# A new hand order for the first 36 positions of a fused attention and two-stage feed-forward kernel, on one core

## Chip, cores and metric

The kernel runs on one core of a Trainium2 chip. The metric is the device time of one execution in microseconds (us), as the median of several executions. The kernel before takes 648.68 us, the median of three runs (647.57 to 649.09).

## What is computed

The reference, cut to its three stages:

```python
# attention: 2 batches, 8 heads, 768 positions, head size 64
scores_l = scale * q @ k.T                    # kept where |i - j| < 16
scores_s = scale * q @ k_sum.T + log(32)      # k_sum: maximum of k over blocks of 32
a = softmax(concat(scores_l, scores_s))
attn = a @ concat(v, v_sum)                   # v_sum: mean of v over blocks of 32
x = attn, heads side by side                  # 1536 x 512
# first feed-forward, d_ff 1536
x = ((x @ w_a) * (x @ w_b)) @ w_out
# second feed-forward, d_ff 2048
h = x @ w_in
out = (h - tanh(h)) @ w_out2
```

The weights arrive as 64-bit floats. The chip's engines turn each tile of them into a 32-bit float by integer work, and each matrix product of the feed-forwards runs as three products of a high and a low part.

## The kernel before

The 1536 rows are taken in three blocks of 512. The first feed-forward walks through each block in "positions": one position is a product with one 128-wide slice of w_a (`pos_a`), w_b (`pos_b`) or w_out (`pos_o`), each of 12 matmuls of 512 columns. Attention is made in 24 units of 64 query positions. Block 0 needs units 0 to 7, block 1 units 8 to 15, block 2 units 16 to 23.

The first 36 positions (`HEAD_P = 36`, line 457), the attention of units 0 to 15 and the decoding of the first 36 weight tiles follow an order written out by hand: the string `SEQ` (line 828). Each name is one step, issued by `op` (line 590 on) in that order. Every engine takes its own steps from the string strictly in their order; steps of different engines only wait for the data and the buffers that they share. After the 36th position the rest comes from a planner's due times and a list scheduler.

Steps on TensorE (PE): `Kt` and `KP` transpose k, `T1t` q, `T2m` makes scores (8 matmuls), `vm` the block means of v, `T3t` transposes the weights of a unit, `T4m` multiplies them with v (16 small matmuls), `Mp0_0` to `Mp35_3` are the quarters of the 36 positions (3 matmuls each).
Steps on ScalarE (ACT): `Ke` evacuates k, `ex` the exponentials, `T4h` the high part of the attention output, `da`/`db` the first two of the decoding steps of a weight tile, `sh` its high part, `Ma`/`Mh` evacuations of positions.
Steps on VectorE (DVE): `Kr` the block maxima of k, `tt` mask and maximum, `rb` the reciprocal of a unit's sum, `T4l` the low part of the attention output, `dd`/`de` (and mostly `df`) the further decoding steps, `Mt`/`Ml`.
For the steps in the table `EC` (line 567) the engine is chosen by a letter (A, D or P for ACT, DVE and GpSimd, which the profile calls POOL): copies of q (`T1ea`, `T1eb`), of k windows (`W`), of transposed weights (`T3e`), the scaling `nm`, copies of the v means `vc`, the decoding step `dc`, the low part `sl` of a weight.
Loads: `LK`, `Lq`, `Lv`, `LV`, `Lk` on the queue of SyncE (SP) for k, q and v; `Lw` for the next weight tile, into one of five staging buffers, when step `df` of an earlier tile has freed it.

A weight's chain is thus `Lw`, `da`, `db`, `dc`, `dd`, `de`, `df`, `sh`, `sl`, and then its position. The first position needs all of `T4h0..7` and `T4l0..7` too, since each product runs over all 512 rows of the block.

PSUM tiles are taken in rotation: eight tags until the eighth unit (`tg`), after that two (`tg2`), so `KP0` takes the place of an earlier `T4m` and waits for its `T4h` and `T4l`.

Dummies: `warm(n, d)` (line 582) puts matmuls that nobody reads ahead of a step. For each unit in `PACED[n]` it issues a small product that reads that unit's sums (so it waits for `rb`) and six transposes of the identity; `FILL[n]` adds single transposes. The steps `T1t`, `T2m`, `T3t` and `T4m` call it; `KP` doesn't:

```python
        elif k == "KP":
            t = knat.pop((1, i))
            pp = pt(tg2(), (128, NP, 128))
            for p in range(NP):
                nc.tensor.transpose(pp[:, p, :], t[:, 2 * p : 2 * p + 2, :], ident)
            P_["KP", i] = pp
```

Of the kernel before, what the change touches and what calls it, by code (L numbers as in the profile page):

```python
# [39 lines left out]
def band_attention_moe_kernel(ctx: ExitStack, tc: tile.TileContext, q, k, v, w_a, w_b, w_out, w_in, w_out2, out):  # L40
# [3 lines left out]
    B, H, S, D = q.shape  # L44
# [530 lines left out]

    qbs = [qbd, qbd2, qbd3, qbd4]
    P_A, P_B = ([j for j in range(HEAD_P) if pos[j][0] is fn] for fn in (pos_a, pos_b))
    FILL = {'KP0': 3}

    SM, PACED = {}, {'T3t0': [5, 3, 0, 1], 'T3t2': [2], 'T3t6': [4], 'T3t7': [6], 'T3t1': [7]}  # L580

    def warm(n, d):
        for u in PACED.get(n, ()):
            mm(d[0:NP, :], SM[u], ident, start=True, stop=True)
            for _ in range(6):
                nc.tensor.transpose(d, ident, ident)  # L586
        for _ in range(FILL.get(n, 0)):
            nc.tensor.transpose(d, ident, ident)

    def op(n):  # L590
# [3 lines left out]
        i, c = int(i or 0), int(c or 0)  # L594
        e = EC.get(n, "A")
        if k == "LK":
# [170 lines left out]
        elif k in ("dc", "dd", "de", "df"):  # L767
# [117 lines left out]
```

## Time and profile before

| | us |
|---|---|
| median of three runs | 648.68 |
| the profiled execution itself | 649.94 |
| its span, first to last instruction | 648.2 |
| TensorE busy in the span | 638.0 (98%) |
| VectorE busy | 499.6 (77%) |
| ScalarE busy | 474.3 (73%) |
| GpSimd busy | 193.4 (30%) |

The span is what the trace covers. Of the profiled execution 1.7 us lie around it. The ends of matmuls in the trace are modelled, so a row of TensorE that overlaps the next is read by its start: the distance from one start to the next is what a step took. The row of a step with three starts or more gives the first start and the end of the last.

### The profile page before, as it was taken

Reading aid. Unit: us, or ns where it says so; the run is one execution under the profiler, and the core shown is the slowest. Engines: PE = TensorE matmul, PEld = TensorE weight load, DVE = VectorE, ACT = ScalarE, POOL = GpSimd, SP = SyncE. Lnnn points to the kernel's source line nnn. Section 1 sums busy time; section 2 is a strip of 40 time slices with the busy share of each in tenths; the row PEclk is TensorE's granted clock in tenths of the full one; section 3 lists DMA queues with packets and bytes.
Section 4 is the critical chain, followed back from the end, with each engine's and each line's share of the span. In section 5 each row is a group of like instructions: output and inputs, shape, how many; then the busy total and the mean of one; then the engine's idle time right before and its main releaser. Section 6 shows DMA issues by size and latency. Waiting matters only on the chain.

```text
span 648.2 us, 9696 instructions
## 1 busy us (share of the span) xinstructions
PE 638.0 (98%) x3296; PEld 521.4 (80%) x3296; DVE 499.6 (77%) x1019; ACT 474.3 (73%) x998; POOL 193.4 (30%) x206
## 2 busy tenths in 40 slices
PE   6999999999999999999999999999999999999997
PEld 5787888778888888888888888888888888888885
DVE  4989999989764777657877748877777877777775
ACT  4889999897676887546555558777777777777774
POOL 5632221110000111001111143544444544444441
PEclk9999999999999999999999999999999999999999
DMA  9979996554514345423444100000010000100001
GB/s 203 252 199 262 252 253 200 173 166 121 148 41 134 123 127 145 143 92 120 147 147 146 34 1 1 0 1 1 2 66 0 1 1 1 50 16 1 1 1 65
DMA packets 81678, 62.12 MB, mean 96 GB/s; under 512 B 45716, under 2 KB 72340, under 8 KB 81628
## 3 DMA queue, kind: packets, MB, share of 16 engines
q1 hardware_dynamic: 79276, 60.32, 33.4%
q0 software_dynamic: 2352, 1.18, 1.5%
q8 instruction: 26, 0.43, 0.3%
q14 instruction: 24, 0.20, 0.1%
HBM read 54.00 MB, written 7.34 MB: 95 GB/s over the span
## 4 chain that ended last, share of the span: by engine, by line
PE 94%; DVE 2%; DMA 2%; SPq 1%; issue 0%; DVEq 0%
PE acc L439 20%; PE pb L350 15%; PE pa L350 15%; PE acc L378 10%; PE acc L802 5%; PE pt L350 5%; PE ps L350 5%; PE pb L808 5%; PE pa L808 4%; PE ps L268 2%; DMA w<-in_q_dram 1%; DMA x20a<-in_q_dram 1%; SPq L597 1%; PE ps L320 1%; PE acc L586 1%; PE pt L268 1%
## 5 line engine op out<-in xcount | busy, mean ns | idle before, releaser
L185 POOL TENSOR_TENSOR wsp<-w,wsp 128x512 fp32r<-128x512 f32 x97 | 127.4, 1331 | 140.1 <-ACT wsp L184 137.7
L184 ACT ACTIVATE wsp<-w 128x512 fp32r<-128x512 f32 x165 | 99.1, 621 | 13.6 <-PE acc L378 8.0
L439 PE MATMUL acc<-wsp,gh 128*128 128x512 f32 x256 | 78.8, 389 | 0.0
L179 POOL TENSOR_SCALAR w<-w 128x512 f32<-128x512 f32 x37 | 25.6, 693 | 171.4 <-ACT w L154 81.4
L185 DVE TENSOR_TENSOR wsp<-w,wsp 128x512 fp32r<-128x512 f32 x68 | 48.6, 715 | 35.8 <-ACT wsp L184 35.5
L378 PE MATMUL acc<-gh,wsp 128*128 128x512 f32 x192 | 64.1, 393 | 0.0
L350 PE MATMUL pa<-XB,wsp 128*128 128x512 f32 x240 | 60.6, 396 | 0.0
L350 PE MATMUL pb<-XB,wsp 128*128 128x512 f32 x240 | 60.4, 394 | 0.0
L343 ACT ACTIVATE gh<-tg 128x512 fp32r<-128x512 f32 x56 | 34.9, 623 | 30.6 <-DVE tg L366 30.3
L439 PEld LDWEIGHTS acc<-wsp,gh 128*128 128x128 f32 x256 | 48.1, 188 | 10.0
L350 PEld LDWEIGHTS pb<-XB,wsp 128*128 128x128 f32 x240 | 44.4, 188 | 9.3
L350 PEld LDWEIGHTS pa<-XB,wsp 128*128 128x128 f32 x240 | 44.1, 188 | 9.3
L439 PE MATMUL acc<-wsp,gl 128*128 128x512 f32 x128 | 49.8, 389 | 0.0
L344 DVE TENSOR_TENSOR gl<-tg,gh 128x512 fp32r<-128x512 f32 x56 | 38.5, 687 | 10.5 <-ACT gh L343 10.3
L439 PE MATMUL acc<-wsp,vw 128*128 128x512 f32 x192 | 46.5, 390 | 0.0
L350 PE MATMUL pa<-XA,wsp 128*128 128x512 f32 x192 | 46.1, 389 | 0.0
L350 PE MATMUL pb<-XA,wsp 128*128 128x512 f32 x192 | 46.1, 389 | 0.0
L439 PEld LDWEIGHTS acc<-wsp,vw 128*128 128x128 f32 x192 | 35.9, 188 | 8.2 <-ACT vw L343 0.4
L350 PEld LDWEIGHTS pb<-XA,wsp 128*128 128x128 f32 x192 | 36.0, 188 | 7.5
L350 PEld LDWEIGHTS pa<-XA,wsp 128*128 128x128 f32 x192 | 36.0, 188 | 7.5
L378 PEld LDWEIGHTS acc<-gh,wsp 128*128 128x128 f32 x192 | 35.8, 188 | 7.5
L378 PE MATMUL acc<-gl,wsp 128*128 128x512 f32 x96 | 37.7, 392 | 0.0
(334 smaller groups left out, 1451.2 us busy)
## 6 DMA issues: line engine op xcount, KB each, us to landing
stage<-in_moe_w_out_dram SPq DMA_DIRECT2D x19, 512.0 KB, 3.3
stage<-in_moe_w_in_dram SPq DMA_DIRECT2D x16, 512.0 KB, 4.5
stage<-in_moe_w_a_dram SPq DMA_DIRECT2D x8, 512.0 KB, 5.6
w<-wsc SPq DMA_DIRECT2D x16, 256.0 KB, 3.5
vw<-in_v_dram SPq DMA_DIRECT2D x19, 192.0 KB, 3.0
stage<-in_moe_w_b_dram SPq DMA_DIRECT2D x7, 512.0 KB, 4.8
wsc<-x21a SPq DMA_DIRECT2D x8, 256.0 KB, 4.5
wsc<-x21b SPq DMA_DIRECT2D x8, 256.0 KB, 4.7
```

Of the source, the lines that this page charges most:

```text
L179: eng.tensor_scalar(rf, rf, HI_HI, HI_LO, op0=ALU.min, op1=ALU.max)
L184: nc.scalar.activation(s[:, 0, :], r, AF.Copy)
L185: eng.tensor_tensor(s[:, 1, :], r, s[:, 0, :].bitcast(F32), op=ALU.subtract)
L268: mm(pp[:, p, 0:NK], qt[:, p, :], kw[:, p, :], start=True, stop=True)
L320: mm(pp[h * 64 : (h + 1) * 64, p * 64 : (p + 1) * 64], vt[:, 2 * p + h, :], at[:, p, h * 64 : (h + 1) * 64], start=True, stop=True,)
L343: nc.scalar.activation(dst[0], src, AF.Copy)
L344: eng.tensor_tensor(dst[1], src, dst[0].bitcast(F32), op=ALU.subtract)
L350: mm(dst, w, xx, start=(kk == 0 and n == 0), stop=(kk == KC - 1 and n == 2))
L378: mm(acc[blk][d][:, c0:c1], w, t, start=(f == 0 and c0 == 0 and n == 0), stop=(f == F1 - 1 and n == 2))
L439: mm(a[c], g[:, cs], s[:, i, :], start=(f == 0 and n == 0), stop=(f == F2 - 1 and n == 2))
L802: mm(acc[0][c], w, t, start=(f == 0 and m == 0), stop=(f == F1 - 1 and m == 2))
L808: mm(P_["M", i], w, t, start=(c == 0 and m == 0), stop=(c == KC - 1 and m == 2))
```

## The change

Three things change: the string `SEQ` (the same 838 steps in another order), 28 letters of the table `EC`, and the two tables of dummies. The diff, with the order cut after the first quarters of the sixth position (the first 20 loads, the same in both, are left out):

```diff
-    EC = {
...
-        'T1eb2': 'D', 'W1': 'D', 'W2': 'P', 'nm0': 'D', 'nm2': 'P', 'T3e2': 'A', 'nm3': 'D', 'nm4': 'P', 'T3e4': 'A', 'nm5': 'P', 'T3e6': 'D',
-        'T3e7': 'D', 'vc1': 'D', 'vc2': 'D', 'vc7': 'P', 'dc7': 'D', 'dc12': 'D', 'dc20': 'P', 'dc23': 'D', 'dc25': 'P', 'dc26': 'P', 'dc28': 'D',
-        'dc29': 'P', 'dc33': 'D', 'W9': 'A', 'W11': 'D', 'T1eb4': 'A', 'nm15': 'D',
...
+    EC = {
...
+        'T1eb2': 'A', 'W1': 'P', 'W2': 'D', 'nm0': 'P', 'nm2': 'D', 'T3e2': 'D', 'nm3': 'P', 'nm4': 'D', 'T3e4': 'D', 'nm5': 'D', 'T3e6': 'A',
+        'T3e7': 'A', 'vc1': 'P', 'vc2': 'P', 'vc7': 'D', 'dc7': 'P', 'dc12': 'P', 'dc20': 'D', 'dc23': 'P', 'dc25': 'D', 'dc26': 'D', 'dc28': 'P',
+        'dc29': 'D', 'dc33': 'P', 'W9': 'D', 'W11': 'A', 'T1eb4': 'D', 'nm15': 'A',
...
-    FILL = {'KP0': 3}
-
-    SM, PACED = {}, {'T3t0': [5, 3, 0, 1], 'T3t2': [2], 'T3t6': [4], 'T3t7': [6], 'T3t1': [7]}
+    FILL = {'KP0': 12, 'T1t4': 1, 'T1t0': 4, 'T1t1': 5, 'T1t2': 5}
+
+    SM, PACED = {}, {'T2m6': [0], 'T3t2': [2, 1], 'T3t4': [4, 3], 'T3t5': [5], 'T3t6': [6, 7]}
...
-    SEQ =
...
-        Kt1 Kt0 Ke0 Kt2 Kt3 Kr1 Kr2 Ke1 W1 Ke2 W0 Kt4 W2 Kr4 Ke3 Kt5 Kr0 Kr3 T1t0 Kr5 W3 Ke4 T1eb0 Lq4 Ws1 T1ea0 T1t1 Ke5 Ws0 Ws2 T2m1 Ws3 T1t2 T2m0 W11
-        T1eb1 tt1 W5 W4 W10 T1ea1 T2m2 va0 T1t3 T2m3 tt0 T1ea2 T1eb2 W7 T2m5 ex1 T2m4 tt2 ex0 T1ea3 ex2 tt3 T1eb3 T2m7 W6 ex3 va1 va2 tt5 tt4 rb2 ex5 T2m6
-        tt7 ex7 vm nm2 tt6 vme T3t2 rb5 rb3 rb0 W8 rb1 nm0 T3t0 ex6 nm3 ex4 T3e0 Lk0 rb7 T3e2 da0 nm1 rb6 T3t3 T3t1 vc1 nm7 db0 T3t7 vc2 rb4 nm6 T3t6 T3e7
-        dc0 nm5 vc0 dd0 T3e3 da1 T3e6 T3t5 de0 dc1 T3e1 LA0 vc3 T4m2 da2 T4m0 vc7 db1 T4m7 vc6 df0 dd1 T4h2 dc2 T4h0 vc5 vc4 de1 dd2 T4l0 T4m3 T4h3 nm4 T4l2
-        T4m6 T4m1 df1 T4l3 T4h7 T4h1 T3t4 T4l1 T3e5 T4m5 T3e4 Lw5 sh0 T4m4 T4h5 T4h6 sl0 T4h4 T1t4 KP0 da4 T4l7 da3 T4l5 db2 T4l6 T4l4 Mp0_0 de2 dc4 T1ea4
-        LA1 Mp0_1 dc3 Mp0_2 sh1 T1eb4 df2 dd3 Lw6 Mp0_3 W9 dd4 T2m8 sl1 Mp1_0 de4 da5 de3 sh2 dc5 KR0 Lw7 Ma0 db3 tt8 dd5 Mp1_1 sl2 Mp1_2 db4 df3 da6 Mp1_3
-        Mp2_0 dc6 KE0 Lq5 sh3 Mt0 db5 df4 LV8 Mp2_1 sl3 Lk1 Mp2_2 da7 dd6 Mp2_3 Lq6 de5 T1t5 Lw8 dc7 Mh0 sh4 Ma1 Mp3_0 db6 df5 sh5 Ml0 Mp3_1 sl4 db7 dd7
-        Mp3_2 de6 ex8 de7 df6 sl5 Lw9 Mp3_3 da8 Mp4_0 Mt1 dc8 T2m9 T1eb5 Mp4_1 Mp4_2 LV9 sh6 rb8 df7 Lw10 dd8 Mp4_3 Mp5_0 Lk2 T1ea5 KP1 Mp5_1
...
+    SEQ =
...
+        Kt0 Kt1 Kt2 Kt4 Kt3 Kt5 Kr2 Ke0 Ke1 Kr1 W2 Ke4 Ke3 Kr0 W0 Kr4 Ke5 T1t0 Kr5 Ke2 Kr3 Ws2 T1t1 T1eb0 Ws0 T1ea0 Ws3 T1t2 T1ea1 T1eb2 W1 Ws1 T2m0 W10 W9
+        W3 T1eb1 tt0 T2m1 T1ea2 tt1 T1t3 T2m3 T2m2 T1ea3 W4 W5 Lk0 va0 T2m4 Lq4 T2m5 tt3 W7 ex0 T1eb3 W6 rb0 T2m6 tt4 ex1 ex3 T2m7 tt5 tt2 ex4 tt6 rb4 rb3
+        nm4 tt7 va1 ex2 va2 nm3 Lk1 rb2 ex6 vm ex7 rb1 nm2 vme T3t4 T3t2 nm1 rb6 T3e4 rb7 nm6 T3t1 T3t3 nm7 vc7 T3e2 ex5 rb5 T3t6 T3e1 vc0 T3e3 T3t7 T3e6 nm5
+        da0 W8 dc0 dd0 nm0 db0 de0 da1 T3t0 dc1 T3e7 df0 T3e0 vc4 dd1 T3t5 vc3 da2 T4m3 dc2 T3e5 vc1 T4m1 de1 T4h3 vc2 T4m4 T4m2 dd2 da3 db1 dc3 vc5 T4h1 de2
+        T4l3 Lw5 vc6 T4m7 T4h7 T4m0 T4m5 T4h4 T4h2 sh0 T4h0 T4l1 T4m6 T4l4 T4l7 T4l2 KP0 T4l0 df1 T4h5 sl0 T4h6 T4l5 db2 da4 T4l6 sh1 db3 dd3 df2 T1t4 Mp0_0
+        T1ea4 W11 dc4 Mp0_1 sl1 Mp0_2 da5 de3 sh2 dd4 df3 Mp0_3 KE0 de4 sl2 T1eb4 KR0 Lw6 Ma0 Lk2 sh3 da6 Mp1_0 Mp1_1 Mp1_2 Mp1_3 db5 Mp2_0 db4 Lw7 Mp2_1 dc5
+        KP1 sl3 Mp2_2 Mp2_3 Lw8 db7 Mt0 dd5 Mh0 df4 de5 Ml0 Mp3_0 da7 sh4 KR1 df5 LV8 Lq5 dc6 Mp3_1 dd6 T2m8 db6 sl4 Mp3_2 Mp3_3 Mp4_0 KE1 Lk3 tt8 de6 da8
+        dc7 Ma1 Lw9 Mp4_1 sh5 db8 T2m9 Lw10 dd7 ex8 df6 Mp4_2 sh6 dc8 da9 sl5 Lk4 dd8 da10 Mp4_3 de7 db9 dc9 Mt1 Mp5_0 tt9 dc10 df7 T1t5 Mh1 Mp5_1
...
```

Taken apart by engine, the part up to the first position reads as follows (a `|` only helps the eye):

```
PE before   Kt1 Kt0 Kt2 Kt3 Kt4 Kt5 T1t0 T1t1 T2m1 T1t2 T2m0 T2m2 T1t3 T2m3 T2m5 T2m4 T2m7 T2m6 vm | T3t2 T3t0 T3t3 T3t1 T3t7 T3t6 T3t5 | T4m2 T4m0 T4m7 T4m3 T4m6 T4m1 T3t4 T4m5 T4m4 | T1t4 KP0 Mp0_0
PE after    Kt0 Kt1 Kt2 Kt4 Kt3 Kt5 T1t0 T1t1 T1t2 T2m0 T2m1 T1t3 T2m3 T2m2 T2m4 T2m5 T2m6 T2m7 vm | T3t4 T3t2 T3t1 T3t3 T3t6 T3t7 T3t0 T3t5 | T4m3 T4m1 T4m4 T4m2 T4m7 T4m0 T4m5 T4m6 | KP0 T1t4 Mp0_0
ACT after   Ke0 Ke1 Ke4 Ke3 Ke5 Ke2 T1eb0 T1ea0 T1ea1 T1eb2 T1eb1 T1ea2 ex0 ex1 ex3 ex4 ex2 ex6 ex7 vme ex5 | T3e1 T3e3 T3e6 da0 db0 da1 T3e7 T3e0 da2 T3e5 T4h3 da3 db1 T4h1 T4h7 T4h4 T4h2 sh0 T4h0 T4h5 T4h6
DVE after   ... tt2 tt6 rb4 rb3 nm4 tt7 rb2 rb1 nm2 nm1 rb6 T3e4 rb7 nm6 nm7 vc7 T3e2 rb5 vc0 nm5 W8 | dc0 dd0 de0 dc1 df0 dd1 dc2 de1 dd2 dc3 de2 T4l3 T4l1 T4l4 T4l7 T4l2 T4l0 T4l5 T4l6
DVE before  ... vc2 rb4 nm6 T3e7 | dc0 vc0 dd0 T3e6 de0 dc1 df0 dd1 dc2 de1 dd2 T4l0 T4l2 T4l3 T4l1 T4l7 T4l5 T4l6 T4l4
```

## Rows read from the trace of the kernel before

**Rows 1.** Stages: stretch and length, then busy us of PE, PEld, DVE, ACT, POOL; clock; DMA

```profile
10.00:13.00 3.00, 1.62 (x11) 1.18 (x12) 2.73 (x8) 1.48 (x3) 0.79 (x2) 1.00 1.36 217
13.00:16.40 3.40, 3.40 (x17) 3.15 (x16) 1.31 (x11) 1.99 (x5) 0.51 (x1) 0.50 1.25 263
26.60:38.60 12.00, 12.00 (x93) 8.86 (x92) 9.49 (x21) 8.63 (x26) 5.70 (x7) 1.00 1.04 292
44.70:167.50 122.80, 122.50 (x697) 98.41 (x696) 118.72 (x281) 109.91 (x256) 21.50 (x28) 1.00 0.78 200
167.50:641.60 474.10, 474.08 (x2245) 391.25 (x2243) 346.27 (x607) 333.59 (x644) 147.71 (x127) 1.00 0.18 56
```

**Rows 2.** Timeline of TensorE at the start: start, length, step [idle before it]

```profile
6.78 0.60 PE L621 MATMUL pb<-ident,XB 128*128 128x128 f32 x4
...
8.98 0.66 PE L621 MATMUL acc<-ident,XB 128*128 128x128 f32 x4 [0.53 <-DMA XB<-in_k_dram]
...
12.69 0.80 PE L652 MATMUL ps<-ident,x20a 128*128 128x128 f32 x4 [0.62 <-DMA x20a<-in_q_dram]
13.35 2.06 PE L268 MATMUL pt<-kw,qbd 128*128 128x120 f32 x8
15.21 1.06 PE L652 MATMUL pa<-ident,x20b 128*128 128x128 f32 x4
```

**Rows 3.** Issue of the load of q for `T1t2` and `T1t3`, on SP's queue

```profile
8.58 2.47 SPq L604 DMA_DIRECT2D x20b<-in_q_dram  x2
```

**Rows 4.** The same load in the list of issues: size, median us to landing

```profile
x20b<-in_q_dram SPq DMA_DIRECT2D x2, 256.0 KB, 5.2
```

**Rows 5.** Timeline of TensorE, two `T2m`, `vm`, and steps with and without dummies

```profile
19.34 1.06 PE L268 MATMUL acc<-kw,XB 128*128 128x120 f32 x8
20.23 1.06 PE L268 MATMUL ps<-kw,XB 128*128 128x120 f32 x8
...
24.00 2.74 PE L747 MATMUL pb<-XA,qn 128*120 128x512 f32 x6
28.23 0.38 PE L584 MATMUL acc<-ident,sm 128*4 128x128 f32 x2
...
32.60 0.60 PE L716 MATMUL acc<-ident,e 128*120 128x128 f32 x4
33.03 0.60 PE L716 MATMUL acc<-ident,ta 128*120 128x128 f32 x4
33.56 0.38 PE L584 MATMUL acc<-ident,sm 128*4 128x128 f32 x2
```

**Rows 6.** All dummy transposes of the execution (line 586), in one stretch

```profile
0.00:648.20 648.20, 6.99 (x48) 5.09 (x48) 1.00 0.35 96
```

**Rows 7.** Timeline of ScalarE: `T3e0` and `da0`

```profile
33.24 0.60 ACT L572 ACTIVATE at<-acc 120x512 f32<-120x512 f32 x1 [2.71 <-PE acc L716]
...
34.21 0.69 ACT L764 ACTIVATE w<-stage 128x512 f32<-128x512 f32 x1
```

**Rows 8.** Timeline of VectorE: last scaling `nm6`, `T3e7`, `dc0`, the last `T4l`

```profile
33.95 0.63 DVE L709 TENSOR_TENSOR w<-w,sm 128x480 f32<-128x480 f32 x1
36.78 0.69 DVE L574 COPY w<-ps 120x512 f32<-120x512 f32 x1 [2.20 <-PE ps L716]
37.39 0.42 DVE L179 TENSOR_SCALAR w<-w 128x512 f32<-128x512 f32 x1
...
44.70 0.41 DVE L740 TENSOR_TENSOR XA<-pb,XA 128x256 fp32r<-128x256 f32 x1
```

**Rows 9.** Timeline of TensorE: first position `Mp0`; `T1t5`

```profile
44.70 3.26 PE L808 MATMUL pa<-XA,wsp 128*128 128x512 f32 x12
...
54.66 0.63 PE L652 MATMUL pt<-ident,w 128*128 128x128 f32 x4 [0.30 <-DMA w<-in_q_dram]
```

**Rows 10.** Timeline of VectorE: the decoding step `dc5`

```profile
49.66 1.53 DVE L179 TENSOR_SCALAR w<-w 128x512 f32<-128x512 f32 x1
```

**Rows 11.** GpSimd in the same stretch: `sl2`

```profile
49.61 1.29 POOL L785 TENSOR_TENSOR wsp<-w,wsp 128x512 fp32r<-128x512 f32 x1 [3.19 <-ACT wsp L782]
```

More of the change, by code (lines that the diff above doesn't have):

```diff
@@ new lines, in band_attention_moe_kernel @@
+    SEQ = 'LK0 LK1 LK2 LK3 LK4 LK5 Lq0 Lq1 Lq2 Lq3 Lv0 Lv1 Lv2 LV0 LV1 LV2 LV3 LV4 LV5 LV6 LV7 Lw0 Lw1 Lw2 Lw3 Lw4 Kt0 Kt1 Kt2 Kt4 Kt3 Kt5 Kr2 Ke0 Ke1 Kr1 W2 Ke4 Ke3 Kr0 W0 Kr4 Ke5 T1t0 Kr5 Ke2 Kr3 Ws2 T1t1 T1eb0 Ws0 T1ea0 Ws3 T1t2 T1ea1 T1eb2 W1 Ws1 T2m0 W10 W9 W3 T1eb1 tt0 T2m1 T1ea2 tt1 T1t3 T2m3 T2m2 T1ea3 W4 W5 Lk0 va0 T2m4 Lq4 T2m5 tt3 W7 ex0 T1eb3 W6 rb0 T2m6 tt4 ex1 ex3 T2m7 tt5 tt2 ex4 tt6 rb4 rb3 nm4 tt7 va1 ex2 va2 nm3 Lk1 rb2 ex6 vm ex7 rb1 nm2 vme T3t4 T3t2 nm1 rb6 T3e4 rb7 nm6 T3t1 T3t3 nm7 vc7 T3e2 ex5 rb5 T3t6 T3e1 vc0 T3e3 T3t7 T3e6 nm5 da0 W8 dc0 dd0 nm0 db0 de0 da1 T3t0 dc1 T3e7 df0 T3e0 vc4 dd1 T3t5 vc3 da2 T4m3 dc2 T3e5 vc1 T4m1 de1 T4h3 vc2 T4m4 T4m2 dd2 da3 db1 dc3 vc5 T4h1 de2 T4l3 Lw5 vc6 T4m7 T4h7 T4m0 T4m5 T4h4 T4h2 sh0 T4h0 T4l1 T4m6 T4l4 T4l7 T4l2 KP0 T4l0 df1 T4h5 sl0 T4h6 T4l5 db2 da4 T4l6 sh1 db3 dd3 df2 T1t4 Mp0_0 T1ea4 W11 dc4 Mp0_1 sl1 Mp0_2 da5 de3 sh2 dd4 df3 Mp0_3 KE0 de4 sl2 T1eb4 KR0 Lw6 Ma0 Lk2 sh3 da6 Mp1_0 Mp1_1 Mp1_2 Mp1_3 db5 Mp2_0 db4 Lw7 Mp2_1 dc5 KP1 sl3 Mp2_2 Mp2_3 Lw8 db7 Mt0 dd5 Mh0 df4 de5 Ml0 Mp3_0 da7 sh4 KR1 df5 LV8 Lq5 dc6 Mp3_1 dd6 T2m8 db6 sl4 Mp3_2 Mp3_3 Mp4_0 KE1 Lk3 tt8 de6 da8 dc7 Ma1 Lw9 Mp4_1 sh5 db8 T2m9 Lw10 dd7 ex8 df6 Mp4_2 sh6 dc8 da9 sl5 Lk4 dd8 da10 Mp4_3 de7 db9 dc9 Mt1 Mp5_0 tt9 dc10 df7 T1t5 Mh1 Mp5_1 db10 T1eb5 Mp5_2 dd10 Mp5_3 Lw11 sl6 LA0 T1ea5 da11 de8 dd9 Ml1 KP2 sh7 Lw12 Mp6_0 Mp6_1 KR2 ex9 Mp6_2 df8 sl7 Mp6_3 KE2 Lq6 dc11 dd11 sh8 db11 Mp7_0 Ma2 de9 KP3 rb8 df9 nm8 Mp7_1 da12 de10 sl8 Mp7_2 LV9 sh9 Lk5 df10 Mp7_3 KR3 KE3 Mt2 Mp8_0 db12 de11 Lw13 T3t8 Lw14 Mh2 sl9 Mp8_1 Mp8_2 df11 T2m10 Lw15 T3e8 da13 dc12 LA1 Ml2 sh10 Lw16 tt10 Mp8_3 sh11 dd12 Mp9_0 da14 rb9 sl10 de12 dc13 sl11 Mp9_1 dd13 ex10 df12 Lq7 Mp9_2 Ma3 rb10 Mp9_3 da15 LA2 de13 Mp10_0 KP4 Mp10_1 KR4 Mp10_2 db15 Mt3 db13 Mp10_3 dc14 Mp11_0 Mp11_1 db14 dc15 sh12 df13 KE4 da16 Mh3 sh13 sl12 db16 Mp11_2 Lw17 W12 nm9 dc16 dd14 Lw18 LV10 dd15 Mp11_3 Mp12_0 de14 dd16 Ma4 nm10 Mp12_1 Ml3 sl13 Mp12_2 da17 de15 df14 da18 df15 de16 Mp12_3 Mp13_0 T3t9 sh14 T2m11 Mp13_1 Mp13_2 Mp13_3 T3e9 Mt4 sh15 tt11 sl14 db18 Lq8 ex11 df16 sh16 Lw19 T4m8 T4h8 Mp14_0 KP5 Mp14_1 dc17 dc18 dd18 Mh4 da19 db17 Lw20 dd17 Mp14_2 W13 sl15 Lq9 db19 Lw21 Mp14_3 de17 rb11 sl16 da20 dc19 T4l8 Mp15_0 Mp15_1 KR5 Mp15_2 LV11 Ml4 Mp15_3 Mp16_0 df17 Ma5 sh17 de18 V12 dc20 df18 T1t6 Mp16_1 Mp16_2 Mp16_3 sl17 dd19 dd20 sh18 Lw22 db20 T1eb6 Mp17_0 de19 da21 Mp17_1 Mp17_2 Lw23 T1ea6 de20 LA3 df19 Mp17_3 KE5 Mt5 sl18 sh19 Lw24 Mp18_0 da22 df20 T2m12 dc21 Mh5 sh20 V13 sl19 dd21 T3t10 Mp18_1 Mp18_2 db21 Mp18_3 dc22 Ml5 da23 de21 tt12 nm11 sl20 Ma6 Mp19_0 dd22 Mp19_1 db22 df21 dc23 T3e10 da24 Mp19_2 Mp19_3 Mp20_0 sh21 de22 Lw25 Mp20_1 da25 Mt6 dd23 Mp20_2 dc24 db24 Mh6 Mp20_3 sl21 df22 de23 Mp21_0 dd24 db23 db25 dc25 de24 ex12 Ma7 T4m9 sh22 T4h9 Lw26 df23 df24 rb12 Mp21_1 Lw27 Ml6 Mp21_2 sl22 dd25 sh24 T3t11 Mp21_3 da26 db26 T4l9 dc26 Mp22_0 mv0 de25 Lw28 nm12 T3e11 W14 sh23 sl24 mv1 dd26 sl23 db27 mvE T2m13 Lw29 Mp22_1 Mp22_2 df25 da27 da28 da29 Mp22_3 Mt7 sh25 dc27 dc28 tt13 Mh7 db29 de26 LV12 Mp23_0 dd28 LM12 df26 W15 T4m10 sh26 Mp23_1 dd27 T4h10 Lw30 Mp23_2 Ml7 ex13 Mp23_3 Mp24_0 T3t12 dc29 sl25 T4l10 de27 de28 T1t7 db30 T3e12 dd29 T1eb7 df27 rb13 T1ea7 Mp24_1 db28 Mp24_2 Mp24_3 Mp25_0 LV13 Ma8 de29 nm13 T4m11 LM13 Lw31 df28 sh27 T2m14 da31 da30 T4h11 Mp25_1 Mp25_2 Mp25_3 sl26 Mt8 dc31 tt14 T4l11 Mp26_0 dc30 dd31 dd30 df29 Mh8 T2m15 Lw32 sl27 ex14 T3t13 tt15 da32 sh29 Mp26_1 sl29 Mp26_2 T3e13 Mp26_3 dc32 T4m12 de30 Mp27_0 Mp27_1 Lw33 Mp27_2 dd32 rb14 sh28 sl28 ex15 db31 rb15 Ml8 T4h12 Lw34 T4l12 df30 T4m13 nm15 Mp27_3 Mp28_0 T4h13 Ma9 nm14 LV14 sh30 T4l13 de31 LM14 sl30 da34 T3t14 T3e14 T3t15 LV15 Mp28_1 T3e15 dc34 df31 db32 T4m14 T4m15 Lw35 T4h15 de32 LV16 Mp28_2 da33 T4l15 T4h14 Mp28_3 Mp29_0 da35 Mp29_1 dc33 Mt9 Mp29_2 T4l14 dd34 dc35 dd33 sh31 db34 LV17 sl31 Mp29_3 Mp30_0 df32 Lw36 Mh9 Mp30_1 dd35 db33 Ml9 sh32 Mp30_2 de33 df33 Mp30_3 de34 Ma10 Mt10 Mp31_0 db35 sl32 Mp31_1 Mp31_2 Mp31_3 Mp32_0 sh33 Mp32_1 Mh10 de35 LV18 df34 Mp32_2 df35 sl33 sh35 Ml10 sl35 Mp32_3 sh34 sh36 sl34 sl36 Ma11 Mp33_0 Mp33_1 Lw37 Mp33_2 Mp33_3 sh37 Mp34_0 Mp34_1 Mt11 sl37 Mp34_2 Mp34_3 Mh11 Ml11 sh38 Mp35_0 Mp35_1 Mp35_2 Mp35_3 sl38 XE0 XE1 XE2 XE3 Lw38'
```

3 lines of the change are left out of this document (1 added, 2 removed).

## The prediction, made before the change was run

> **What bounds the kernel now.** I read the busy time by stages first, then TensorE's timeline from its start to the first position, then the timelines of VectorE and ScalarE beside it, and last the few waits that are left. The stages show that TensorE has work in 474.08 of the 474.10 us after the 36th position and in 122.50 of the 122.80 us between the first position and the end of the hand order [rows 1]. All the matmuls stay in the change, so time can only come from two places: how early the first position starts, 44.70 us in the profile [rows 9], and waits inside the 122.80 us. There the reader should see one wait, 0.30 us for a load of q [rows 9], and that VectorE is busy for 118.72 us [rows 1]: TensorE sets the pace and VectorE keeps up with 4.1 us to spare.
>
> Before the first position TensorE looks full too, 12.00 of 12.00 us between 26.60 and 38.60 [rows 1], but part of this are dummies. There are 48 of the transposes on line 586 [rows 6], which is eight groups of six; a group with its small product takes (32.60 - 28.23) / 4 = 1.09 us [rows 5]. They are meant to run while TensorE would wait for the softmax. They run longer: `T3e0` on ScalarE came after 2.71 us of idleness that TensorE ended [rows 7], and VectorE, done with its last scaling at 33.95 + 0.63 = 34.58, idled 2.20 us until TensorE gave it unit 7 at 36.78 [rows 8]. So in this stretch the dummies are on the path. From `dc0` at 37.39 VectorE then runs without a gap to the last `T4l` at 44.70, and the first position starts with that [rows 8, 9].
>
> **The change, part by part.** *Number of dummies.* PACED names eight groups in both kernels, one of them now ahead of `T2m6`. FILL goes from 3 to 27, but 12 of these (and the 3 of before) belong to `KP0`, whose branch never calls `warm`; the 48 records of before, all of them of the groups, bear it out [rows 6]. So 15 are added: 14 between the q transposes, where TensorE waits for loads (idle 0.62 us ahead of `T1t1` [rows 2], room for five at 0.43 / 4 = 0.11 us, the pitch of a transpose [rows 5]), and one ahead of `T1t4`.
>
> *Up to `vm`.* After the change `T1t2` precedes all scores. Its q is issued at 8.58 and takes 5.2 us [rows 3, 4]: 13.78, so `T1t2` runs at 13.8 and `T2m0` begins at 14.25 (a transpose step takes 33.03 - 32.60 = 0.43 us [rows 5]). Nothing holds the scores up from here: ScalarE's copies of q start when `T1t0` is done, as before. Eight `T2m` of 20.23 - 19.34 = 0.89 us, `T1t3` of 0.43 and one group of 1.09 end at 22.9; `vm`, 2.7 us [rows 5], ends at 25.6, where it began at 24.00 and ended at 26.7 before: 1.1 us ahead. This holds if the clock stays up. In the trace it was at 0.50, the lower level, from 13.00 to 16.40, after three microseconds with 1.62 us of work [rows 1], and `T2m1` took 15.21 - 13.35 = 1.86 us [rows 2] where 0.89 is usual. I take it as staying up, because the 14 dummies lie just there. The other end, the same 3.4 us at the lower level, is the first rival. The Trainium skill (TensorE: Matmul & The Clock Gate, Part 1) says that the slow clock is the default and that activity lifts it; by that rule the idle time opened by taking `Kt4` ahead of `Kt3` speaks against this change, the dummies for it.
>
> *From `vm` to `dc0`.* TensorE is to run two groups and `T3t4`, two and `T3t2`, `T3t1`, `T3t3`, two and `T3t6`. Six groups at 1.09 are 6.5 us, five transposes at 0.43 are 2.2, and the switch into a group costs 0.1 (33.56 - 33.03 = 0.53) [rows 5]: `T3t6` starts at 34.0 and ends at 34.5. The scalings that these steps need were done at 34.58 at the latest before [rows 8], and they begin sooner now, with the scores; again the dummies are what is waited for. ScalarE copies unit 6 (34.6 to 35.2), then runs `da0` of 0.69 us [rows 7], and `dc0` starts on VectorE at 35.95, against 37.39 before [rows 8]. That is 1.4 us gained.
>
> *From `dc0` to the first position.* Before, 44.70 - 37.39 = 7.31 us [rows 8]. After, two steps leave this stretch, `vc0` and `T3e6`, and two come, `dc3` and `de2`, a short and a long one each time (a `dc` 0.42 us, a copy 0.61 to the next start [rows 8]); I count 7.3 us at most. The last `T4l` starts at 43.2 and ends at 43.6 [rows 8]. What it waits for is just in time: ScalarE's seventeen steps behind `da0` (ten of some 0.55 us, seven `T4h` of some 0.3, by their rows' pitch) bring `T4h6` to 43.1, and `sl0` on GpSimd, 1.3 us as `sl2` [rows 11], ends at 43.6. TensorE has finished `T4m6` at 41 and runs `KP0` and `T1t4` as their PSUM places come free, the latter after `T4l0` (43.0) with one dummy: 43.05 + 0.11 + 0.43. The first position then starts at 43.6, which is 1.1 us earlier than 44.70 [rows 9].
>
> *Inside the 36 positions.* `T1t5` moves from the end of the third position to the sixth, some 6 us later, and its load is not issued later by as much: its 0.30 us go [rows 9]. The letters of EC move net one `dc` to GpSimd and some copies from ScalarE to VectorE and back; the cover for them is TensorE's own 122.80 us, and if it were gone each would cost about a `dc`, 0.42 us [rows 8]. TensorE switches to small steps 25 times where it did 27 times; I take that as nothing. `LA0`, which stood on SP's queue ahead of `Lw5`, moves behind the sixth position, and the three loads that add to it follow; what waits for them, `mv0`, stands behind the 22nd position in both, so sixteen positions of 2.7 us cover it.
>
> The sum: -1.1 - 0.3 = -1.4 us. Against the profiled execution that is 649.94 - 1.4 = 648.5. The median of the runs is 1.26 us below that execution, and the same 1.4 off the median gives 647.3.
>
> **The rivals.** *The clock falls all the same (or did not fall in the runs that set the median).* For it speaks the new pause from 6.78 + 0.43 = 7.2 to 8.98, in which the kernel before had `Kt3` [rows 2]; against it that the waits behind it are filled. TensorE's chain from `T2m0` to `T3t6` has no slack, so half speed from 13.0 to 16.4 costs at least 1.86 - 0.89 = 1.0 us, and with the rest of the stretch 1.4. Nothing but the 0.3 us is left: 648.4, no change.
>
> *VectorE falls behind the positions: slower.* Positions 1 to 3 now follow with only a transpose between, where `T2m8`, `T1t5` and `T2m9` gave VectorE time. VectorE has 4.1 us of idle time in the whole stretch [rows 1], and an earlier start of 1.1 us takes that much of them. The place is a `dc` on VectorE beside a step of GpSimd: `dc5` took 1.53 us where `dc0` took 0.42, and it ended just after `sl2` on GpSimd did [rows 8, 10, 11]. 1.1 us each; three such steps more than before use up what is left, and from the fourth on TensorE waits. With five, and one load of a weight late by as much, TensorE loses 2.2 + 1.1 = 3.3 us, and with the 1.4 gained the kernel takes 648.68 - 1.4 + 3.3 = 650.6. Against it: the new order has df2 right behind the `T4l`, so staging buffers are freed sooner than before. The Trainium skill (SBUF — State Buffer, "SBUF: two separate sides") calls this port an exclusive lock between the two engines, and the row agrees.
>
> *More than I count.* The first position lasted 3.26 us [rows 9] where twelve matmuls without a wait take 2.7; if `T4l6` and `sl0` are there in time, 0.4 us more go, and without the lower clock in any run the gain reaches 2.5 us: 646.2.
>
> **How the numbers follow.** What a measurement of this kernel can tell from no change is about 0.2%, 1.3 us. My forecast has a chance of 0.45 (its own range 646.6 to 648.1, so a good part of it lies at the bound), the clock 0.25, VectorE behind 0.18, more than I count 0.12. Faster by over 1.3 us is most of the first and all of the last, 0.47; slower is the third, 0.18; the rest, 0.35, is no change. The range reaches from 645.8 to 649.6: it leaves out the worse half of the slower case and the end of the best.
>
> **What would show it.** Right: 63 transposes on line 586; a granted clock of 1.00 from 10 to 20 us; `T3t6` near 34, `dc0` near 36, the first position near 43.6; no wait for a load at `T1t5`; the distance from the first position to the end some 0.3 us shorter. A clock of 0.50 in the first 20 us shows the first rival, waits of TensorE for `wsp` on VectorE or ScalarE after 45 us the second. The prediction is wrong if the dummies are not what TensorE is busy with between `vm` and `T3t6`, or if another load holds the first decodings.

## The result, and the profile after

The changed kernel takes 652.41 us (median of six executions, 651.11 to 653.95), the kernel before beside it 648.88 us (six, 647.57 to 649.52): a ratio of 1.0053, 95% interval 1.0037 to 1.0069. It is 3.5 us slower, and the forecast was 1.4 us faster. The profiled execution takes 652.65 us, its span is 650.9 us.

First the stages, cut where the kernel after has its first position and the end of the hand order (stretch and length, then busy time of PE, PEld, DVE, ACT and POOL, then the granted clock and the DMA's share and rate):

```profile
10.00:13.00 3.00, 2.78 (x22) 2.22 (x22) 2.13 (x5) 2.75 (x6) 0.83 (x2) 1.00 1.35 218
13.00:16.40 3.40, 3.40 (x31) 3.16 (x30) 2.08 (x17) 2.69 (x6) 0.51 (x1) 1.00 1.22 262
26.60:38.60 12.00, 12.00 (x122) 9.48 (x124) 11.04 (x24) 7.32 (x22) 4.78 (x7) 1.00 1.14 296
44.04:167.80 123.76, 123.76 (x716) 100.92 (x715) 117.56 (x293) 114.09 (x275) 25.10 (x28) 1.00 0.76 201
167.80:644.30 476.50, 472.86 (x2227) 389.52 (x2225) 345.94 (x591) 327.94 (x626) 149.83 (x127) 1.00 0.18 55
```

Beside [rows 1] this reads: the clock is 1.00 from 10 us on where before it was 0.50 between 13.00 and 16.40; the hand-ordered part has no idle time of TensorE left; but behind it TensorE has work in only 472.86 of 476.50 us, 3.64 us short, where before 0.02 us were missing. That last row belongs to code that the diff doesn't touch.

TensorE's timeline at the start, with the steps that the prediction named (start, length, what it is, idle time before it; the row behind `T1t2` is the first `T2m`):

```profile
13.10 0.71 PE L588 MATMUL pt<-ident 128*128 128x128 f32 x5
13.81 0.66 PE L652 MATMUL pt<-ident,x20b 128*128 128x128 f32 x4
14.31 1.05 PE L268 MATMUL pa<-kw,qbd 128*128 128x120 f32 x8
...
23.54 2.74 PE L747 MATMUL pb<-XA,qn 128*120 128x512 f32 x6
...
34.56 0.60 PE L716 MATMUL ps<-ident,w 128*120 128x128 f32 x4
...
42.86 0.65 PE L635 MATMUL ps<-ident,w 128*128 128x128 f32 x4 [1.39 <-DVE XA L740]
...
44.04 3.00 PE L808 MATMUL pa<-XA,wsp 128*128 128x512 f32 x12
```

`T1t2` runs at 13.81, `vm` ends at 26.2, `T3t6` runs at 34.56, and the first position starts at 44.04, 0.66 us ahead of [rows 9]. That is 0.44 us later than the forecast's 43.6, and most of the 3.5 us is lost elsewhere.

Where, the list of TensorE's waits says. In the stretch from 160 to 300 us the kernel before has none at all; after (what waits, for what; us in total, times, longest):

```profile
PE pt L307 <- ACT e L300: 2.7, 2, 2.1
PE pt L307 <- DVE e L297: 0.9, 1, 0.9
```

Line 307 transposes the softmax weights of a unit of block 2, lines 300 and 297 scale them. One of the three places in ScalarE's timeline shows what they wait for:

```profile
236.12 0.58 ACT L310 ACTIVATE at<-pt 120x512 f32<-120x512 f32 x1
238.98 0.66 ACT L155 ACTIVATE stage<-stage 128x512 int32<-128x512 uint32 x1 [2.29 <-DMA stage<-in_moe_w_in_dram]
239.59 0.66 ACT L154 ACTIVATE x21b<-stage 128x512 f32<-128x512 f32 x1
240.16 0.38 ACT L283 ACTIVATE e<-e,nm 128x120 f32<-128x120 f32 x1
...
242.74 1.25 ACT L300 ACTIVATE e<-e,sm 128x120 f32<-128x120 f32 x4 [0.46 <-DVE sm L295]
```

And VectorE's last row maximum of that unit, and TensorE beside it:

```profile
237.67 0.08 DVE L279 DVE_READ_ACCUMULATOR2_ANT nm<- 128x1 f32 x1
...
240.36 0.69 PE L320 MATMUL ps<-at,vw 120*64 120x64 f32 x16
243.18 1.18 PE L307 MATMUL pt<-ident,e 128*120 128x128 f32 x4 [2.14 <-ACT e L300]
```

VectorE had the unit's row maxima ready at 237.7. ScalarE was then standing at line 155, the decoding step of a tile of w_in that came next in its order, until that tile's load had landed at 238.98. The exponentials of line 283 stood behind it in ScalarE's order and came at 240.16; the scaling ended at 243.99, and the transposes that wait for it were next in TensorE's order. The Trainium skill (TensorE: Matmul & The Clock Gate, table at its head) says that ScalarE takes its queue strictly first in, first out; the 2.29 us agree. The 3.6 us in the list agree with the 3.64 us by which the stage is short (an expectation below puts these waits at 5.0 us; the list has 3.6). The transposes also stretch at this place, 1.18 us where 0.62 is usual, which the rows count as work.

### The profile page after: what moved, and what is told of

It reads as the page before. It is cut to its first block, busy times and chain, and to the rows that moved or that the text cites. A ratio compares the mean times of both kernels' runs of the same rounds, so it can differ in the third digit from the quotient of the medians.

```text
span 650.9 us, 9723 instructions
## 1 busy us (share of the span) xinstructions
PE 637.8 (98%) x3311; PEld 522.4 (80%) x3311; DVE 499.8 (77%) x1017; ACT 474.2 (73%) x1002; POOL 198.8 (31%) x207
## 3 DMA queue, kind: packets, MB, share of 16 engines
q0 software_dynamic: 2352, 1.18, 1.5%
HBM read 54.00 MB, written 7.34 MB: 94 GB/s over the span
## 4 chain that ended last, share of the span: by engine, by line
PE 78%; DMA 7%; ACT 5%; SPq 5%; DVE 3%; issue 2%; ACTq 0%; DVEq 0%
PE acc L439 20%; PE pb L350 11%; PE pa L350 11%; PE acc L378 7%; DMA stage<-in_moe_w_in_dram 6%; PE pb L808 5%; PE pa L808 5%; PE pt L350 5%; PE ps L350 5%; PE acc L802 4%; SPq L238 2%; DMA w<-in_k_dram 1%; ACT e L283 1%; ACT wsp L184 1%; ACT stage L155 1%
## 5 line engine op out<-in xcount | busy, mean ns | idle before, releaser
L179 POOL TENSOR_SCALAR w<-w 128x512 f32<-128x512 f32 x38 | 30.5, 819 | 176.2 <-ACT w L154 94.7
```

The costliest lines, as they stand in the source:

```text
L179: eng.tensor_scalar(rf, rf, HI_HI, HI_LO, op0=ALU.min, op1=ALU.max)
```

## The experiments

Theory 1 was that the new head is as good as forecast and that the list scheduler, which orders positions 36 to 71 behind it, made the loss. Theory 2 was that the new head leaves a backlog that is only paid there (the prediction's second rival, later).

**The two heads with each other's order behind.** The order that was compiled for one kernel is laid on the other, for all engines but SyncE, whose order is fixed in both. It needs no change of the computation, only edges of order between the instructions of positions 36 to 71 (`ORDER` holds their numbers, by engine):

```diff
...
+    for eng, ks in ORDER.items():
+        ks = [int(x) for x in ks.split()]
+        for a, b in zip(ks, ks[1:]):
+            tc.add_manual_dep(I[n36 - 1 + b], I[n36 - 1 + a].name, same, reason="order")
...
```

The first of the two runs also keeps what the old order has behind the hand-ordered part behind it: unit 16's first transposes come at 165.92 us there, as late as in the kernel before, and at 151.42 us in the kernel after.

> The kernel after the change, but each engine's instructions of positions 36 to 71 are held in the order that the kernel before was compiled to. Theory 1 (the new head is about 1 us faster, and the loss of about 4 us is made by the order that the list scheduler found for positions 36 to 71 behind the new head): 647.2 to 648.4 us, no waits of TensorE's transposes on line 307 between 160 and 300 us, and the lead of 0.65 us at the first position is kept to the end. Theory 2 (the new head leaves ACT, VectorE or the loads behind, and positions 36 to 71 only pay that back): 651.5 to 653 us, TensorE waits there as in the kernel after.

Measured: 648.79 us against 649.05, ratio 1.0005 (0.9996 to 1.0014), and no wait of line 307. The loss is gone with the order, so theory 2 falls: the new head carries no backlog that an order of the rest could not hide. But the time is not below the kernel before either, and it is above the 647.2 to 648.4 us of theory 1. The head's own gain isn't there.

> The kernel before the change, but each engine's instructions of positions 36 to 71 are held in the order that the kernel after was compiled to. Theory 1 (the order of positions 36 to 71 makes the loss): 652 to 654 us, with TensorE waiting on line 307 for the exponentials. Theory 2 (a backlog left by the new head makes it): 648.3 to 649.5 us, no such waits.

Measured: 660.67 us, ratio 1.0179 (1.0161 to 1.0198): 12 us slower, and not the 3 to 5 that theory 1 gave. TensorE's waits between 160 and 300 us:

```profile
PE pa L350 <- ACT ta L358: 3.6, 1, 3.6
PE ps L268 <- DVE nm L279: 1.5, 1, 1.5
PE pt L307 <- ACT e L300: 1.3, 2, 0.8
PE ps L268 <- ACT qbd L253: 1.3, 1, 1.3
PE pt L307 <- DVE e L297: 1.2, 1, 1.2
```

Three of the five are of other kinds than in the kernel after. That order has units 16 and 17 started inside the hand-ordered part; behind the old head unit 16's first transposes come at 165.54 us and not at 151.42. That this costs the rest is argued and not tested (the five waits are 8.9 of the 12 us). So an order can be worse behind another head than behind its own, and this run supports theory 1 in its direction alone.

**No list scheduler at all.** `REG` says from which position on which engines keep the program's order: SyncE from 36, all from 72. Here all keep it from 36 on, in both kernels:

```diff
-    REG = {36:{ET.SP},72:None}
+    REG = {36:None}
```

> The kernel after the change, with positions 36 to 71 in program order on every engine, as positions from 72 on are. To be read against the old head with the same edit: theory 1 expects this kernel 0.5 to 1.5 us below it, theory 2 expects it 3 us or more above it. Against the kernel before neither theory gives a number: program order may cost waits of its own in both, some 0 to 30 us.

> The kernel before the change, with positions 36 to 71 in program order on every engine. The control of the new head with the same edit: theory 1 expects it 0.5 to 1.5 us above that one, theory 2 expects it 3 us or more below.

Measured: 660.66 us (659.78 to 662.21) and 661.43 us (660.36 to 661.49). With one and the same order behind, the new head is 0.8 us below the old, which is inside the spread of either: theory 2 fails again, and the gain is small at best. What the list scheduler is worth here is about 12 us, so it can't just be left out.

**The kernel before, profiled once more.**

> The kernel before the change, profiled once more. If the fall of the granted clock to 0.50 at 13.0 to 16.4 us in the profile of before belongs to the kernel (as the prediction took it): the same window shows 0.50 again, and the first position begins near 44.7 us. If it belonged to that one execution: 1.00 in that window, and the first position near 43.2 us, as in the two profiles of the old head with another order behind it.

Measured: 649.17 us, span 647.5. The stages, and the steps of TensorE and VectorE that the prediction was built on:

```profile
10.00:13.00 3.00, 1.48 (x10) 1.04 (x11) 2.87 (x8) 1.36 (x3) 0.97 (x3) 1.00 1.35 217
13.00:16.40 3.40, 3.38 (x30) 3.15 (x30) 2.11 (x17) 3.32 (x9) 0.81 (x2) 1.00 1.22 261
43.35:166.75 123.40, 122.45 (x697) 98.54 (x696) 118.41 (x281) 110.06 (x257) 22.38 (x28) 1.00 0.77 199
166.75:641.00 474.25, 474.23 (x2245) 391.26 (x2243) 346.29 (x607) 333.43 (x644) 148.18 (x127) 1.00 0.18 56
```

```profile
13.47 1.15 PE L268 MATMUL pt<-kw,qbd 128*128 128x120 f32 x8
...
43.35 3.26 PE L808 MATMUL pa<-XA,wsp 128*128 128x512 f32 x12
...
53.70 0.63 PE L652 MATMUL pt<-ident,w 128*128 128x128 f32 x4 [0.64 <-DMA w<-in_q_dram]
```

```profile
36.05 0.41 DVE L179 TENSOR_SCALAR w<-w 128x512 f32<-128x512 f32 x1
```

The same program, and no fall of the clock, although TensorE had only 1.48 us of work in the three microseconds ahead, less than the 1.62 of [rows 1]. `T2m1` takes 14.46 - 13.47 = 0.99 us to the next start instead of 1.86, `dc0` comes at 36.05 instead of 37.39 [rows 8], and the first position at 43.35 instead of 44.70. The fall belonged to the one execution that had been profiled. In the four groups of runs below and above the kernel before was timed 70 times beside the others; 60 of these show a mean clock of 0.999 or more (median 648.83 us) and 10 one of 0.997 or less (median 650.29). So a lower mean clock goes with 1.46 us and is in one execution of seven, and the median of before hardly contains it. Only the mean is on record for these executions: that the ten fell in the same place, at 13 to 16.4 us, isn't shown. Nor are they spread evenly: 8 are among 32 on one chip, 2 among 23 on a second, none among 15 on a third.

**Without the dummies on line 588.**

```diff
-    FILL = {'KP0': 12, 'T1t4': 1, 'T1t0': 4, 'T1t1': 5, 'T1t2': 5}
+    FILL = {'KP0': 3}
```

> The kernel after the change with the old count of dummies on line 588 (three, at KP0, of 27), the order of all else as it was. If the dummies keep the clock up: 0.50 somewhere between 10 and 17 us in at least some executions, the first position 0.5 to 1.5 us later, 652.5 to 654 us. If they do nothing: 652.0 to 652.8 us, clock 1.00.

Measured: 652.26 us (652.04 to 652.65; the kernel after had 652.41). The count at `KP0` has no effect in either, since that step doesn't run them; so this takes away all 15. The first position starts at 44.07. The clock stays up without them:

```profile
10.00:13.00 3.00, 1.70 (x12) 1.10 (x11) 2.65 (x6) 2.75 (x6) 0.96 (x2) 1.00 1.36 217
13.00:16.40 3.40, 2.82 (x26) 2.61 (x25) 2.01 (x15) 2.63 (x6) 0.51 (x1) 1.00 1.23 260
```

They cost nothing and bring nothing that four executions show. They don't prevent the fall in every execution either. The first of the three tries below has the same steps and the same dummies up to the scores, and in its profile TensorE waits 1.72 us for a load of k until 9.25 us, ahead of all dummies, and the clock is at 0.50 from 10 to 12 us:

```profile
10.00:13.00 3.00, 3.00 (x17) 3.00 (x16) 0.95 (x2) 2.08 (x4) 0.35 (x1) 0.56 1.33 219
```

That pause is the one that the prediction's first rival named. Whether the dummies make a fall rarer is left open (in the kernel after two of six executions have a mean clock of 0.996; where it fell in those isn't on record). Without them the trace shows what they cover, the load of q that `T1t2` waits for:

```profile
13.97 0.63 PE L652 MATMUL pt<-ident,x20b 128*128 128x128 f32 x4 [0.58 <-DMA x20b<-in_q_dram]
```

In the new order the first scores stand behind this step. They begin at 14.31 us in the kernel after, and at 13.47 in the kernel before with the clock up, where `T2m1` runs while the load is on its way.

**Only ScalarE's queue.** The kernel after with its own compiled order held, and in it eight instructions moved by a few places: at three units the waiting decoding (630, 747, 854 and 791: four instructions, not the five of the expectation) goes behind the unit's exponentials, at a fourth the row maxima (797 to 803) go ahead. In the numbers of `ORDER`:

```diff
-    Activation: ... 630 ... 460 462 563 464 466 ...
+    Activation: ... 460 462 563 464 466 630 ...
-    Activation: ... 747 ... 570 679 572 451 574 576 ...
+    Activation: ... 570 679 572 451 574 576 747 ...
-    Activation: ... 854 791 686 688 690 692 ...
+    Activation: ... 686 688 690 692 854 791 ...
-    DVE: ... 626 874 875 652 915 797 799 801 803 ...
+    DVE: ... 797 799 801 803 626 874 875 652 915 ...
```

> The kernel after the change, every engine's order of positions 36 to 71 held as it was compiled, but for five ACT instructions and one group on VectorE: at three units the decoding that waits for a w_in load (line 155; at the third also the line 154 behind it) moves behind the unit's eight exponentials (line 283), and at a fourth unit the row maxima of line 279 move ahead of the differences and decodings that stand before them. Theory 1a (the loss is ACT's in-order queue: exponentials that are ready stand behind a decoding whose load has not landed, so the transposes of line 307 come late): the waits of 5.0 us at line 307 go to below 1 us, and the time to 648 to 649.2 us. Theory 1b (the loads are late as such, and whatever stands behind them on ACT or VectorE will be late): the wait only changes its place, 651 to 652.5 us.

> The run with the exponentials first, without its change on VectorE: only the three decodings on ACT (and the line 154 behind the third) move behind their unit's exponentials. Theory 1a: the waits at line 307 at about 217 and 241 us go (together 3.8 us in the profile of the kernel after), the one at about 256 us, whose row maxima stand behind decodings on VectorE, stays (1.1 us): 649 to 650.2 us. Theory 1b: 651 to 652.5 us.

Measured: 648.72 us (ratio to before 1.0004, 0.9994 to 1.0014) with all of it, and 648.66 us (0.9993, 0.9981 to 1.0004) with ScalarE's part alone. Moving four instructions on ScalarE brings back the whole 3.7 us. Nothing else differs: between 150 and 330 us the traces of this run and of the kernel after have the same order on every engine but for these four, so the holding of the order isn't what helps. Between 160 and 300 us TensorE waits, with all of it,

```profile
PE pt L307 <- DVE e L297: 0.3, 1, 0.3
PE pt L307 <- ACT e L300: 0.3, 1, 0.3
```

and the place shown above now reads on ScalarE:

```profile
235.82 0.40 ACT L283 ACTIVATE e<-e,nm 128x120 f32<-128x120 f32 x1 [0.47 <-DVE nm L279]
...
237.35 0.66 ACT L155 ACTIVATE stage<-stage 128x512 int32<-128x512 uint32 x1
237.91 0.65 ACT L154 ACTIVATE x21b<-stage 128x512 f32<-128x512 f32 x1
```

The exponentials wait for their own row maxima, and the decoding behind them finds its load landed. Theory 1b falls: the wait didn't just change its place. But the load itself also comes earlier. SyncE issued it at 233.00 in the kernel after and at 230.49 here:

```profile
233.00 0.37 SPq L141 DMA_DIRECT2D stage<-in_moe_w_in_dram  x1
230.49 0.37 SPq L141 DMA_DIRECT2D stage<-in_moe_w_in_dram  x1
```

It goes out when VectorE has finished the decoding that frees the staging buffer (that step begins at 232.24 and at 229.73), and VectorE itself stood behind ScalarE at the unit before (3.74 us idle there in the kernel after, 0.92 here). So a decoding that stands in front of ready work makes the next load later too; how much of the 3.7 us either part gives wasn't separated. One number missed: with ScalarE alone the wait at 256 us was to stay, and only 0.3 us of it did; the rest had come from the delays before it.

**The early start of units 16 and 17.** In the kernel after the scheduler had moved the first transposes of block 2 (line 249) from 167.51 to 151.42 us, into the hand-ordered part. This run holds them back and lets it order anew:

```diff
...
+    last = next(i for i in reversed(I[:n36]) if i.engine == ET.PE)
+    first = next(i for i in I[n36:] if i.engine == ET.PE)
+    tc.add_manual_dep(first, last.name, mybir.DependencyInfo(mybir.DependencyClass.NoSync, mybir.DependencyReason.DATA), reason="order")
```

> The kernel after the change, where unit 16's transposes (line 249) may not be issued before TensorE's last instruction of the 36 hand-ordered positions; the list scheduler orders the rest anew. In the kernel after they ran at 151.6 us, in the kernel before at 167.6 us. Theory 1c (the loss comes of units 16 and 17 being pulled into the hand-ordered part, so that their successors' exponentials meet the w_in loads): 648 to 649.2 us and no waits at line 307. If the early start is not what matters, and any order that the scheduler finds can fall this way: anything from 648 to 654 us, with waits at line 307 as the order has it.

Measured: 648.21 us, ratio 0.9997 (0.9988 to 1.0006), no wait of line 307, and TensorE busy without a gap:

```profile
166.00:284.00 118.00, 118.00 (x675) 96.90 (x674) 77.37 (x196) 82.84 (x202) 9.59 (x15) 1.00 0.39 118
```

With the early start barred the scheduler finds an order without the loss, here and in the three tries below: from line 249's first transposes to the last matmul it is 472.0 to 472.7 us in all four. That supports the early start as what led it to the bad order; that any other disturbance would have done the same isn't excluded. The early start isn't bad by itself: in the run with the exponentials first the units start as early (155.2 us for the first scores) and nothing is lost. Which step of `SEQ` opened the place for it wasn't tried.

**Three tries at a faster first position.** All on the kernel with the units held back. In the kernel after TensorE waits 1.39 us at `KP0` for the first `T4l`, which stand behind decodings on VectorE. The steps of `SEQ` between `T4m1` and `Mp0_0` are moved (the dummies at `KP0`, 12 or 3, never run):

```diff
-T4m2 dd2 da3 db1 dc3 vc5 T4h1 de2 T4l3 ... KP0 T4l0 df1 T4h5 sl0 T4h6 T4l5 db2 da4 T4l6 sh1
+T4m2 dd2 vc5 T4h1 T4l3 ... KP0 T4l0 T4h5 T4h6 T4l5 T4l6 db1 df1 sl0 da3 dc3 de2 db2 da4 sh1
```

> The kernel with unit 16's transposes held back, and a change in the new order of the first positions: the decodings da3, db1, dc3 and de2 move behind the last T4h and T4l, and the dummies at KP0 go from 12 to 3. In the run with the units held back TensorE waited 1.4 us at KP0 for the first half result on VectorE (line 740), which began at 41.29 us behind decodings. If the first position waits only for those copies: it begins near 42.5 us (43.9 before), and the time is 647.0 to 647.8 us. If the decodings that move back are then late for positions 1 to 4: the lead of about 1.3 us is gone by the fifth position, 648 to 649 us.

Measured: 652.03 us, ratio 1.0032 (1.002 to 1.0044), above both ranges. The profiled execution is the one with the low clock at the start shown above, so its scores begin at 15.08 us, not at 14.31. The wait at `KP0` is down to 0.46 us, but the first position itself stops for `sl0`, which stands on GpSimd behind `df1` and so behind the `db1` that was moved:

```profile
42.70 0.66 PE L635 MATMUL ps<-ident,w 128*128 128x128 f32 x4 [0.46 <-DVE XA L740]
...
43.89 0.71 PE L808 MATMUL pa<-XA,wsp 128*128 128x512 f32 x2
46.64 1.57 PE L808 MATMUL pa<-XA,wsp 128*128 128x512 f32 x3 [2.04 <-POOL wsp L785]
```

> As units_late_x_first, but only da3, dc3 and de2 move behind the first half results; db1, df1 and sl0, for which TensorE waited 2.0 us there, stay where the change has them, and so do the 12 dummies. If the first position waits for the copies into XA and the displaced decodings have slack: the wait at KP0 shrinks from 1.4 to about 0.8 us, the first position begins near 43.3 us, and the time is 647.2 to 648.2 us. If positions 2 and 3 then wait for their weights: 648.5 to 650 us.

Measured: 649.67 us, ratio 1.001 (0.9997 to 1.0023). The first position starts at 43.28 as expected, with 0.62 us of waiting left at `KP0`, but against the run with the units held back (43.94) the lead of 0.66 us is used up: the 19th position starts at 102.88 us against 102.31, and the last matmul comes 1.0 us later than there. The third position still has the lead (48.88 against 49.52 us) and stops for its low part, which comes from GpSimd:

```profile
49.66 1.19 PE L808 MATMUL pa<-XA,wsp 128*128 128x512 f32 x4 [0.17 <-POOL wsp L785]
```

The fourth starts at 52.52 against 52.71, so 0.45 us of the lead go here: the second condition of the expectation. What costs the rest, up to the 19th position, wasn't followed up.

> As units_late_x_first, but sh0 and sl0 move ahead of the halves T4h and T4l, and db1, df1, da3, dc3 and de2 behind them; the 12 dummies stay. If position 1's weights are ready in time all the same: the first position begins near 42.7 us, and the time is 646.8 to 647.8 us. If position 1 waits for sl1 (df1 on POOL takes its place behind db1): up to 2 us at about 46 us, 648.5 to 650.5 us.

Measured: 652.68 us, ratio 1.0056 (1.0035 to 1.0078), above both ranges. With `sl0` ahead, a copy of the v means on GpSimd comes late, and TensorE waits 1.96 us for it before a `T4m`:

```profile
42.47 0.69 PE L728 MATMUL pa<-gl,vw 120*64 120x64 f32 x16 [1.96 <-POOL vw L755]
```

This profile is of the fastest of six executions (650.84 us), so it explains only a part of the 652.68.

No version found here beats the kernel before; the four without the loss equal it (648.21 to 648.79 us, ratios 0.9993 to 1.0005).

## Why the prediction was wrong

- **The step that failed: "All the matmuls stay in the change, so time can only come from two places".** It read 474.08 of 474.10 us in [rows 1] as a property of the stretch behind position 36. It was a property of the order that a scheduler had found for the old head. That order is worked out again whenever the head changes; the new one lost 3.6 us to ScalarE's queue, and the runs with another order behind the new head get them back. Neither the forecast nor a rival named this place. The rival of VectorE falling behind had the direction but another mechanism: TensorE has no idle time in the hand-ordered part after (123.76 of 123.76 us), VectorE keeps up.
- **The second failure: the clock's 1.1 us.** The mechanism was right for the profiled execution and wrong for the median. The working took the start of the first position, 44.70 us, from an execution whose clock had fallen, gained 1.1 us against it, and then subtracted the same 1.4 us from a median of runs 1.26 us below that execution. That surplus is about what a lower clock goes with in the timed executions, 1.46 us (the two profiled executions of before are only 0.77 us apart). With the clock up the old head starts its first position at 43.35, so the forecast's own 43.6 was no gain. What the low clock hid is the price of taking `T1t2` ahead of the scores: `T2m0` at 14.31 instead of a first score at 13.47, and the same delay stands at `vm` (23.54 against 22.67). The first rival said so in a parenthesis ("or did not fall in the runs that set the median") and with its 648.4 it gives what the new head is worth: 648.2 to 648.8 us with a good order behind it.
- **Dummies as the path from `vm` to `T3t6`: about right.** `T3t6` forecast at 34.0, measured at 34.56. The difference lies ahead of `vm`'s end (26.2 where 25.6 was forecast), 0.48 us of it one wait of the first group for its sum's reciprocal; from there it is 8.4 us, as forecast. The dummies are on line 586 (48) and 588 (15), not all on 586 as the prediction put it.
- **`dc0` at 35.95: measured 36.37.** Undisturbed, the old head has it at 36.05: no gain. The stretch behind it came out as counted: 7.34 us to the start of the last `T4l` (43.71) where 7.3 was the most, and 7.67 us to the first position (44.04) where 43.6 - 35.95 = 7.65 was forecast. So it starts 0.69 us later than the old head's 43.35. Over all profiles with the clock up at the start: 43.16 to 43.35 in three of the old head, 43.78 to 44.24 in seven of the new one with its steps in this order.
- **The load wait at `T1t5`: right in kind, too small.** It is gone; undisturbed it was 0.64 us, not 0.30. The hand-ordered part as a whole has 0.95 us less idle time (122.45 of 123.40 us before), which pays for the later start: the head is level.
- **The sum as measured**, between the two profiled executions with the clock up, 650.9 - 647.5 = 3.4 us: 0.69 later at the first position, 0.95 less idle time up to position 36, 3.6 more behind it, together 3.3. (Some 1.3 us of TensorE's work moved from the last stage into the one ahead; it cancels.)
- **The last rival** adds 1.4 and 0.4 us and comes to 2.5. No row stands behind the other 0.7 us; the first position itself takes 0.26 us less than before (3.00 for 3.26 us).

## What to carry to other kernels

A part of a program that a scheduler orders by its own model is not fixed by leaving its source alone: after any change ahead of it, compare the compiled order and the waits there first, and hold the old order to tell a loss of the change from a loss of the reordering. In an in-order queue an instruction that waits for a load belongs behind the work that is ready and that another engine waits for; such moves at three units were worth 3.7 us here, the earlier loads included. And before a gain is taken from one profiled execution, check whether its surplus over the median of the runs is the very thing that the gain removes.

## What the runs showed of the hardware

The granted clock at the start differs between executions of one program: 0.50 from 13.00 to 16.40 us in one profile of the kernel before, 1.00 in the next with less work of TensorE ahead of it. The Trainium skill (TensorE: Matmul & The Clock Gate, Part 1) says that the chip's observation of activity runs freely and does not begin anew with a kernel; two outcomes of one program agree with that. Behind a stop later on the outcome differs too, in two different kernels. The 2.04 us wait of the first try above, with 1.59 us of work in the three around it, was followed by a stretch partly at the lower level (stretches as in the tables of stages):

```profile
43.00:46.00 3.00, 1.59 (x11) 0.96 (x9) 2.66 (x5) 3.00 (x7) 2.14 (x2) 1.00 0.00 0
46.00:50.00 4.00, 3.36 (x8) 2.71 (x9) 4.00 (x6) 3.19 (x7) 1.77 (x2) 0.59 0.95 221
```

The 2.14 us wait in the kernel after, with 1.04 us of work in three, was not:

```profile
240.00:243.00 3.00, 1.04 (x18) 0.55 (x17) 1.21 (x5) 2.54 (x11) 0.61 (x1) 1.00 0.00 0
243.00:247.00 4.00, 3.82 (x17) 2.88 (x18) 2.54 (x4) 2.55 (x7) 0.00 (x0) 1.00 0.82 208
```

Of either kernel two of six executions have a mean clock of 0.995 or 0.996 and the other four 0.999 or more, so here too it changes from one execution to the next; where it fell is on record only for the first try's profiled one, once at the start and once behind this wait.
